# A spatial-reduction attention kernel: the query scratch in 16 rows, chunks of neighbouring tokens

## The chip, the core and the metric

The kernel runs on one core of a Trainium2 chip. The core has a matrix engine (TensorE, PE in the profile, with its weight loads as PEld), VectorE (DVE), ScalarE (ACT), GpSimd (POOL), and a queue processor (SyncE, SP) that here only issues transfers. Sixteen DMA engines move the data of the queues of SP, ACT and POOL. The metric is the time on the device in microseconds (us), of one execution. The median of three runs before is 380.58 us (380.52 to 380.81).

## What is computed

Attention of 4 x 12288 queries over 768 pooled keys per batch, followed by a mixture of eight low-rank adapters of which two are chosen for each token. The reference, cut to what matters:

```python
B, C, Hh, Ww = (4, 128, 384, 32)       # q: B x 12288 x 128, kv: B x 384 x 32 x 128
kv_pool = kv.reshape(B, H // r, r, W // r, r, C).mean(axis=(2, 4))     # r = 4
kv_flat = kv_pool.reshape(B, -1, C) @ w_sr
k = v = kv_flat                                                       # 768 keys
s = scale * (q @ k.transpose(0, 2, 1))
s = s - s.max(-1, keepdims=True)
a = np.exp(s)
a /= a.sum(-1, keepdims=True) + 1e-09
x = (a @ v)                                                           # 49152 x 128
logits = x @ w_gate                                                   # E = 8
topk = the two largest;  w = softmax over those two
out = x + sum over the two of  w * ((x @ A[e]) @ B[e])                # rank 16
```

Every token is computed by itself; the order in which tokens are taken is free, as long as each result reaches its own row of the output.

## The kernel before

**Chunks and groups.** The 49152 tokens are taken in 96 chunks `k` of T = 512 tokens, 24 per batch, and four chunks make a group `g` of GT = 2048 tokens (24 groups). A chunk has S = 4 strips of 128 tokens, the 768 keys J = 6 blocks of 128.

**Queries.** TensorE needs the queries transposed, channels on partitions: `qT[g]`, 128 x 2048 bf16. For groups 0 and 1 the queries are loaded as fp32 and turned on TensorE (`load_q`, `turn_q`). For the other 22 groups `cast_q` (L78) copies 2048 tokens from the input to a scratch tensor in DRAM, from fp32 to bf16, on POOL's queue (L80), and `load_qT` (L83) reads it back with a transposing DMA on SP's queue (L90). It sees the scratch as 128 rows `p` of 16 tokens `j` (2048 elements), so column `j*128 + p` of `qT` is token `16 p + j`. A chunk thus holds, for each of 128 partitions, four neighbouring tokens out of 16, and takes tokens from the whole group. The cast of group 4 + i is issued in the slots 8, 12, ..., 60 and in six more (`casts`, L463), the load of group g in slot 4g - 6 for g = 4 to 17, and the last six in slots 61 to 67 (`loads`, L464). A slot is one turn of the main loop, `begin(k)`; the attention of chunk k - 1 and the routing and adapters of earlier chunks are done in it. The last four groups' `qT` lie in a spare buffer (`qTs`).

**Scores.** `scores(k, r)` (L286) multiplies two blocks of keys with the chunk's 512 columns into a PSUM tile `sg` of 2 x 512, and ScalarE takes the exponential of all 1024 columns at once (L294) into `em[k]`, a tile of [128 keys, J, T] fp16. Three such units make a chunk; the main loop calls `unit()` at fixed places, somewhat more than a chunk ahead of the attention. There are two `sg` buffers.

**Attention.** `attend(k, s)` (L296) uses a strip of `em` as weights: for each of the 6 key blocks a 128 x 128 load of `em[k][:, j, s*128:(s+1)*128]` and a matmul with the extended values (136 columns) into `acc`. So the tokens of a strip come out on the partitions. `normalize` (L313), `top` and `route` choose the adapters. `attend_part` (L305) does the same in the opening, and `part` (L676) at the end.

**Adapters.** `transposes` turns x and the gated hidden values on TensorE; for the chunks in `by_dma` (68 to 89) `turn_dma` (L405) does it with transposing DMAs on SP's queue. `tanhs` runs the tanh of the routing on ScalarE (L365).

**Output.** `finish(k)` (L431) adds up and stores 256 KB on SP's queue (L434), out of one of eight `osb` buffers: 128 partitions with 2 KB each, which in the output lie 8 KB apart. At the end of the kernel, after the loop, the last chunks are stored by `add_there` (L709, two whole chunks) and `add_here` (L699, one whole chunk and four halves), the latter also on ACT's queue; both use `dest(k)` (L695).

**Order.** `keep` makes each instruction stay in program order on its engine; the queues are served in order, and waits between engines go by semaphores.

Of the kernel before, what the change touches and what calls it, by code (L numbers as in the profile page):

```python
# [11 lines left out]
BF16 = mybir.dt.bfloat16  # L12
U16 = mybir.dt.uint16
FP16 = mybir.dt.float16
AF = mybir.ActivationFunctionType
# [5 lines left out]
def kernel(  # L21
# [10 lines left out]
    nc = tc.nc  # L32
    P = 128
    B, N, C = q.tensor.shape
# [3 lines left out]
    J = NKV // P  # L38
    T = 512
    S = T // P  # L40
    GC = 4
    GT = GC * T
    VC = C + E - 1
    VE = VC + 1
    VP = 2 * C
    NB = N // T
    NCHUNK = B * NB
    scale = 1.0 / float(np.sqrt(C))
# [6 lines left out]
    ppool = ctx.enter_context(tc.tile_pool(name="ppool", bufs=8))  # L55
# [5 lines left out]
    qdram = ctx.enter_context(tc.tile_pool(name="qdram", bufs=1, space=bass.MemoryType.DRAM))  # L61
# [4 lines left out]
    keep = tc.keep_in_program_order  # L66

    def mm(*a, **k):
        return keep(nc.tensor.matmul(*a, **k))  # L69
# [5 lines left out]
    NG = N // GT  # L75
    q_bf, qT, kvr, spare = {}, {}, {}, {}

    def cast_q(g):  # L78
        t = qdram.tile([GT, C], BF16, tag=f"q{g}", name=f"qbf{g}")
        keep(nc.gpsimd.dma_start(t, q[g // NG, (g % NG) * GT:(g % NG + 1) * GT]))  # L80
        q_bf[g] = t

    def load_qT(g):  # L83
        if g < B * NG - GC:
            t = qpool.tile([P, GT], BF16, tag="qT", name="qT")
        else:
            if "q" not in spare:
                spare["q"] = kvpool.tile([P, 4, 2, 4 * C], FP32, tag="kvr", name="qTs")
            t = spare["q"][:, g % GC].rearrange("p x c -> p (x c)").bitcast(BF16)
        keep(nc.sync.dma_start(t.rearrange("c (j p) -> c j p", p=P),  # L90
                               q_bf[g].rearrange("(p j) c -> p (j c)", p=P), transpose=True))
        qT[g] = t


# [113 lines left out]
    kfT, vx = {}, {}  # L208
# [73 lines left out]
    em, acc, xn, xg, srt, gw = {}, {}, {}, {}, {}, {}  # L282
    tts, xT, hgT, hp, hg, dp = {}, {}, {}, {}, {}, {}
    R = J // 2

    def scores(k, r):  # L286
        b = k // NB
        if k not in em:
            em[k] = ppool.tile([P, J, T], FP16, tag="em", name="em")
        rhs = qT[k // GC][:, (k % GC) * T:(k % GC + 1) * T]  # L290
        ps = ps_s.tile([P, 2, T], FP32, tag="sg", name="sg")
        for i in range(2):
            mm(ps[:, i], kfT[b][:, 2 * r + i], rhs, start=True, stop=True)
        keep(nc.scalar.activation(em[k][:, 2 * r:2 * r + 2], ps, AF.Exp, bias=0.0, scale=scale))  # L294

    def attend(k, s):  # L296
        b = k // NB
        if s == 0:
            acc[k] = ps_a.tile([P, S, 256], FP32, tag="acc", name="acc")
        o = acc[k][:, s, 0:VE]  # L300
        for j in range(J):
            mm(o, em[k][:, j, s * P:(s + 1) * P], vx[b][:, j, 0:VE], start=(j == 0),
               stop=(j == J - 1))

    def attend_part(k, r):  # L305
        if r == 0:
            acc[k] = ps_a.tile([P, S, 256], FP32, tag="acc", name="acc")
        for s in range(S):
            for j in (2 * r, 2 * r + 1):
                mm(acc[k][:, s, 0:VE], em[k][:, j, s * P:(s + 1) * P], vx[k // NB][:, j, 0:VE],  # L310
                   start=(j == 0 and s % 2 == 0), stop=(j == J - 1 and s % 2 == 1))

    def normalize(k):  # L313
# [112 lines left out]
    def up(k):  # L426
        dp[k] = mtile([P, S, C], name="d_ps")
        for s in range(S):
            mm(dp[k][:, s], hgT[k][:, s], b_bf, start=(s == 0), stop=(s == S - 1))

    def finish(k):  # L431
        osb = opool.tile([P, S, C], FP32, tag="osb", name="osb")
        keep(nc.vector.tensor_tensor(osb, dp[k], xn[k][:, :, 0:C], op=ALU.add))  # L433
        keep(nc.sync.dma_start(  # L434
            out[k // GC * GT:(k // GC + 1) * GT].rearrange("(p j) c -> p j c", p=P)
            [:, k % GC * S:(k % GC + 1) * S], osb))
        for d in (em, acc, xn, xT, hgT, hp, hg, dp):
            d.pop(k, None)

# [9 lines left out]
    def cast_first():  # L449
        keep(nc.gpsimd.tensor_copy(late, q_f[1, 2][:, 0, 0:1]))  # L450
        for g in (2, 3):
            cast_q(g)
        for g in (2, 3):
            load_qT(g)
# [3 lines left out]
    def unit(k=None, r=None):  # L458
        k, r = units.pop(0 if k is None else units.index((k, r)))
        scores(k, r)  # L460
# [7 lines left out]
    def begin(k):  # L468
        nonlocal sums, rest
        b, i = divmod(k, NB)  # L470
        g = k // GC
        if k in loads:
            load_qT(loads[k])
        if k in casts:
            cast_q(4 + casts.index(k))
        if b + 1 < B:
            lo = 3 if b == 0 else 0
            if i == lo:
                sums, rest = prepare(b + 1, nc.gpsimd)
                sums = sum(sums, [])  # L480
            if lo <= i < 12 + lo:
                load_kv(b + 1, (i - lo) // 4, (i - lo) % 4, None)
        if k == 7:
            for _ in range(2):
                sums.pop(0)()
# [11 lines left out]
    enter, t, left = {}, 1, list(range(NCHUNK - 3))  # L497
# [10 lines left out]
    def step(op, *w):  # L508
        v = [int(x) if x.isdigit() else engines.get(x, pools.get(x)) for x in w]
        if op == "T":  # L510
            turn_rows(v[0], 2 * (v[2] // 2) if w[1] == "s" else v[2],
                      v[2] % 2 if w[1] == "s" else v[3])
        elif op == "turn":
            turn_q(v[0] // GC, v[0] % GC, *v[1:])
        elif op in ("keys", "keys2", "values"):
            first_rest[v[0]][("keys", "keys2", "values").index(op)]()
        elif op == "gates":
            later.pop(0)()
        else:
            {"spin": spin, "proj1": project, "proj2": project2, "sum": add_rows, "sc": unit,  # L520
             "late": cast_first, "cast": cast_weights, "slot": begin, "at": attend, "atp": attend_part,
             "norm": normalize, "top": top, "route": route, "tr": transposes, "down": down,
             "gate": gate, "up": up, "fin": finish}[op](*v)
# [23 lines left out]
    for k in range(k1, NCHUNK):  # L547
        b, i = divmod(k, NB)
# [11 lines left out]
        if kx and not kd and all(x_ in by_dma for x_ in kx):  # L560
# [16 lines left out]
            for u_ in ku:  # L577
                up(u_)
                finish(u_)
            attend(ka[0], 0)  # L580
            attend(ka[0], 1)
            unit()
            for n in kn:
# [25 lines left out]
        for u_ in ku:  # L609
            up(u_)  # L610
            finish(u_)
# [64 lines left out]
    def part(k, o, js):  # L676
        for s in range(S):
            for j in js:
                mm(o[:, s, 0:VE], em[k][:, j, s * P:(s + 1) * P], vx[k // NB][:, j, 0:VE],
                   start=(j == 0 and s % 2 == 0), stop=(j == J - 1 and s % 2 == 1))  # L680

    def wide(o):
# [9 lines left out]
        for s in range(S):  # L692
            mm(o[:, s], hgT[k][:, s], b_bf, start=(s == 0), stop=(s == S - 1))

    def dest(k):  # L695
        return out[k // GC * GT:(k // GC + 1) * GT].rearrange("(p j) c -> p j c", p=P)[
            :, k % GC * S:(k % GC + 1) * S]

    def add_here(k, lo, hi, queue):  # L699
        osb = opool.tile([P, S, C], FP32, tag="osb", name="osb")[:, 0:hi - lo]  # L700
        keep(nc.vector.tensor_tensor(osb, dp[k][:, lo:hi], xn[k][:, lo:hi, 0:C], op=ALU.add))
        keep(queue.dma_start(dest(k)[:, lo:hi], osb))

    def carry(k):
        osb = opool.tile([P, S, C], FP32, tag="osb", name="osb")
# [2 lines left out]

    def add_there(k):  # L709
        keep(nc.gpsimd.tensor_tensor(dp[k], dp[k], xn[k][:, :, 0:C], op=ALU.add))  # L710
        keep(nc.sync.dma_start(dest(k), dp[k]))

    def gate_part(k, lo, hi):
        if lo == 0:
# [8 lines left out]
    up_into(K - 4, bank(ps_m))  # L723
    o95 = bank(ps_s).rearrange("p a (b c) -> p (a b) c", c=256)
    part(K, o95, range(4))
    fetch(xT, K - 2)
    tanhs()
    down_into(K - 2, ps_m)
    carry(K - 4)
    normalize(K - 1)  # L730
    turn_x(K - 1, ps_m)
    part(K, o95, range(4, J))
    turn_h(K - 3, ps_a)
    fetch(xT, K - 1)
    top(K - 1)
    route(K - 1)
    gate_part(K - 2, 0, S)
    add_there(K - 4)

    acc[K] = o95  # L740
# [26 lines left out]
    fetch(hgT, K - 2)  # L767
    carry(K - 3)
    add_there(K - 3)
    halves = [(K, 0), (K, 2), (K - 1, 0), (K - 1, 2)]  # L770
    for k, lo in halves:
# [13 lines left out]
    for k, lo in halves:  # L785
        half(turned[k], lo, hg[k], id_bf, True)
        keep(nc.scalar.copy(hgT[k][:, lo:lo + 2], turned[k][:, lo:lo + 2]))
        if (k, lo) == (K, 2):
            half(dp[K], 0, hgT[K], b_bf, False)
            add_here(K - 2, 0, S, nc.sync)  # L790
        elif k < K:
            if lo == 0:
                half(dp[K], 2, hgT[K], b_bf, False)
                add_here(K, 0, 2, nc.sync)
                add_here(K, 2, S, nc.sync)
# [35 lines left out]
```

## Time and profile before

| | |
|---|---|
| median of the runs | 380.58 us (380.52 to 380.81, n = 3) |
| span of the profiled execution | 379.1 us |
| PE busy | 368.8 us, 97% |
| VectorE busy | 307.6 us, 81% |
| ScalarE busy | 293.3 us, 77% |
| GpSimd busy | 217.8 us, 57% |
| DMA | 82.22 MB, mean 217 GB/s |

The profile is of one execution. Its span runs from the first to the last instruction that the profiler recorded; the time of a run holds 1.5 us more. A group of instructions is shown as line, engine, operation, output<-input, number, then busy time and mean in ns, then the idle time before and what ended it. A line of the timeline has the start, the length, and what ran (neighbours of one kind are merged, xN). A line of the issues has the queue, the number, the size and the time from issue to landing.

### The profile page before, as it was taken

What the parts mean: (1) busy time and instruction counts of PE and PEld (TensorE: products, weight loads), DVE (VectorE), ACT (ScalarE), POOL (GpSimd) and SP (SyncE); (2) the same over time, 40 slices, a digit from 0 to 9 for tenths busy, and PEclk for the clock granted to TensorE, in tenths of its full rate; (3) what the DMA queues carried; (4) which work ended last, traced back from release to release, by engine and by line L of the source; (5) the groups of instructions that cost most, each with busy time, mean ns of one, the idle gap of its engine ahead of it and who ended that gap; (6) DMA issues with size and microseconds to landing.
All of it is one profiled execution on the core that took longest, in us unless ns stands there. A gap on an engine that the chain in (4) does not pass through costs nothing.

```text
span 379.1 us, 11473 instructions
## 1 busy us (share of the span) xinstructions
PE 368.8 (97%) x4448; PEld 292.5 (77%) x4448; DVE 307.6 (81%) x925; ACT 293.3 (77%) x368; POOL 217.8 (57%) x493
## 2 busy tenths in 40 slices
PE   8899999999999999999999999999999999999993
PEld 5577788788788887878788887878787777777782
DVE  1447799998989889898989888898988777777785
ACT  1448986776878788787878787777778999999873
POOL 0120468878732387777833267777675666666442
PEclk9999999999999999999999999999999999999998
DMA  7988979999999998997898998989955867777623
GB/s 247 388 291 151 279 184 266 340 224 241 152 213 228 299 278 268 255 235 165 171 201 226 288 239 245 306 233 198 217 137 140 169 163 153 150 205 168 141 86 140
DMA packets 93863, 82.22 MB, mean 217 GB/s; under 512 B 73104, under 2 KB 73872, under 8 KB 93456
## 3 DMA queue, kind: packets, MB, share of 16 engines
q1 hardware_dynamic: 92672, 69.75, 69.8%
q0 software_dynamic: 704, 11.54, 17.0%
q8 instruction: 35, 0.57, 0.6%
q10 hardware_dynamic: 432, 0.20, 0.2%
q14 instruction: 20, 0.16, 0.2%
HBM read 50.53 MB, written 36.70 MB: 230 GB/s over the span
## 4 chain that ended last, share of the span: by engine, by line
PE 91%; DMA 4%; DVE 2%; issue 1%; ACT 1%; SPq 0%; POOL 0%; ACTq 0%; DVEq 0%; POOLq 0%
PE acc L69 35%; PE sg L69 32%; PE tt_ps L69 8%; PE d_ps L69 5%; PE h_ps L69 5%; DMA kvr<-in_kv_dram 4%; PE kpT_ps L69 2%; PE v_ps L69 1%; DVE kvr L135 1%; DVE xn L320 1%; PE kfT_ps L69 1%; DMA out_dram<-osb 1%; PE qT_ps L69 0%; SPq L102 0%; PE tail_ps L69 0%
## 5 line engine op out<-in xcount | busy, mean ns | idle before, releaser
L294 ACT ACTIVATE em<-sg 128x1024 f16<-128x1024 f32 x288 | 282.4, 1022 | 66.8 <-PE sg L69 64.1
L69 PE MATMUL acc<-vx,em 128*128 128x136 f16 x2280 | 166.5, 223 | 0.0
L69 PEld LDWEIGHTS <-em 128*128 128x128 f16 x2304 | 145.2, 98 | 7.7 <-DVE xn L320 0.4
L69 PE MATMUL sg<-qT,kfT 128*128 128x512 bf16 x480 | 142.1, 379 | 0.8 <-ACT em L294 0.7
L320 DVE TENSOR_TENSOR xn<-acc,rinv 128x540 f32<-128x540 f32 x95 | 68.4, 720 | 3.3
L69 PEld LDWEIGHTS <-tts 128*128 128x128 bf16 x564 | 43.0, 98 | 31.6 <-issue 0.4
L223 POOL TENSOR_TENSOR kvr<-kvr 128x512 f32<-128x512 f32 x54 | 67.3, 1270 | 0.1
L352 POOL TENSOR_TENSOR over<-xn,srt 128x64 f32<-128x64 f32 (+1 forms) x120 | 30.9, 278 | 55.4 <-DVE srt L340 55.3
L433 DVE TENSOR_TENSOR osb<-d_ps,xn 128x512 f32<-128x512 f32 x91 | 62.5, 688 | 0.0
L420 DVE TENSOR_TENSOR hg<-h_ps,gw 128x512 bf16<-128x512 f32 x71 | 49.0, 691 | 6.3 <-POOL gw L368 1.2
L389 DVE COPY tts<-tt_ps 128x1024 bf16<-128x1024 bf16 (+1 forms) x73 | 49.0, 672 | 0.0
L69 PEld LDWEIGHTS <-kfT 128*128 128x128 bf16 x576 | 45.3, 98 | 2.7 <-issue 1.0
L315 DVE RECIPROCAL rinv<-acc 128x4 f32<-128x4 f32 x95 | 17.3, 182 | 36.9 <-PE acc L69 35.9
L367 POOL TENSOR_TENSOR gw<-th,over 128x64 f32<-128x64 f32 (+1 forms) x60 | 17.3, 288 | 49.6 <-ACT th L365 47.4
L69 PEld LDWEIGHTS <-xn 128*128 128x128 bf16 x296 | 22.5, 98 | 16.7 <-DVE xn L320 0.4
L340 DVE MAX8 srt<-xn 128x8 f32<-128x8 f32 x380 | 34.4, 152 | 0.1
L69 PE MATMUL sg<-qTs,kfT 128*128 128x512 bf16 x96 | 28.6, 379 | 0.0
L69 PE MATMUL tt_ps<-id_bf,xn 128*128 128x128 bf16 x284 | 27.4, 219 | 0.0
L69 PE MATMUL h_ps<-a_bf,tts 128*128 128x128 bf16 x284 | 27.4, 219 | 0.0
L69 PE MATMUL tt_ps<-id_bf,hg 128*128 128x128 bf16 x280 | 27.1, 219 | 0.0
L69 PE MATMUL d_ps<-b_bf,tts 128*128 128x128 bf16 x276 | 26.7, 219 | 0.1
L358 POOL TENSOR_SCALAR over<-over 128x64 f32<-128x64 f32 (+1 forms) x60 | 19.8, 330 | 5.4
(93 smaller groups left out, 280.7 us busy)
## 6 DMA issues: line engine op xcount, KB each, us to landing
out_dram<-osb SPq DMA_DIRECT2D x94, 256.0 KB, 4.3
kvr<-in_kv_dram SPq DMA_DIRECT2D x45, 512.0 KB, 7.8
qbf<-in_q_dram POOLq DMA_DIRECT2D x22, 512.0 KB, 7.7
qf<-in_q_dram SPq DMA_DIRECT2D x8, 256.0 KB, 7.4
kvr<-in_kv_dram SPq DMA_DIRECT2D x6, 256.0 KB, 7.8
out_dram<-osb SPq DMA_DIRECT2D x3, 128.0 KB, 2.3
turn<-turn SPq DMA_TRANSPOSE x23, 3.1
qT<-qbf SPq DMA_TRANSPOSE x18, 7.4
```

Of the source, the lines that this page charges most:

```text
L69: return keep(nc.tensor.matmul(*a, **k))
L223: keep(adder.tensor_tensor(u[:, lo:hi], u[:, lo:hi], v[:, lo:hi], op=ALU.add))
L294: keep(nc.scalar.activation(em[k][:, 2 * r:2 * r + 2], ps, AF.Exp, bias=0.0, scale=scale))
L315: keep(nc.vector.reciprocal(ri, acc[k][:, :, VC]))
L320: keep(nc.vector.tensor_tensor(x[:, :, 0:VC], acc[k][:, :, 0:VC], ri.unsqueeze(2).broadcast_to([P, S, VC]), op=ALU.mult))
L340: keep(nc.vector.max(srt[k0][:, m, s], xn[k][:, s, C:C + E]))
L352: keep(eng.tensor_tensor(d, lg, so[:, :, i].unsqueeze(2).broadcast_to([P, n, 8]), op=ALU.subtract))
L358: keep(eng.tensor_scalar(mask, mask, 0.0, None, op0=ALU.is_ge))
L367: keep(eng.tensor_tensor(w[:, 0:n], th, mask, op=ALU.mult))
L389: keep(nc.vector.tensor_copy(sb[:, lo:hi], ps[:, lo:hi]))
L420: keep(nc.vector.tensor_tensor(hg[k].rearrange("p s (e r) -> p (s e) r", e=E), hp[k].rearrange("p s (e r) -> p (s e) r", e=E), gw[k0][:, m ...
L433: keep(nc.vector.tensor_tensor(osb, dp[k], xn[k][:, :, 0:C], op=ALU.add))
```

## The change

Three things go together, for groups 2 to 23 (chunks 8 to 95).

The scratch tensor of a group has 16 rows `r`. Row r holds, for each of the four chunks m of the group, 32 neighbouring tokens (8 KB in bf16): token `512 m + 32 r + x` of the group. The transposing DMA reads the 16 rows as they are, so column `512 m + 16 x + r` of `qT` is that token, and a chunk is 512 neighbouring tokens.

`em[k]` is laid out as [keys, strip, key block, 128]. The exponential reads the scores in another order: with `x = 4 u + s`, strip s takes the columns `64 u + 16 s + r`, in runs of 16. A strip's partition `16 u + r` is then token `32 r + 4 u + s` of the chunk, so a partition has four neighbouring tokens in its four strips. In groups 0 and 1 the strips are read as before, in runs of 128.

The store (a new function `store`, used for all outputs) writes 128 runs of 2 KB into the chunk's own 256 KB of the output, in the order u, r; groups 0 and 1 are stored as before.

```diff
     def cast_q(g):
-        t = qdram.tile([GT, C], BF16, tag=f"q{g}", name=f"qbf{g}")
-        keep(nc.gpsimd.dma_start(t, q[g // NG, (g % NG) * GT:(g % NG + 1) * GT]))
+        t = qdram.tile([16, GT // 16 * C], BF16, tag=f"q{g}", name=f"qbf{g}")
+        src = q[g // NG, (g % NG) * GT:(g % NG + 1) * GT]
+        keep(nc.gpsimd.dma_start(t.rearrange("r (m x) -> r m x", m=GC),
+                                 src.rearrange("(m r x) c -> r m (x c)", r=16, m=GC)))
         q_bf[g] = t
...
-        keep(nc.sync.dma_start(t.rearrange("c (j p) -> c j p", p=P),
-                               q_bf[g].rearrange("(p j) c -> p (j c)", p=P), transpose=True))
+        keep(nc.sync.dma_start(t.rearrange("c (i r) -> c i r", r=16), q_bf[g], transpose=True))
...
     def scores(k, r):
         b = k // NB
         if k not in em:
-            em[k] = ppool.tile([P, J, T], FP16, tag="em", name="em")
+            em[k] = ppool.tile([P, S, J, P], FP16, tag="em", name="em")
...
-        keep(nc.scalar.activation(em[k][:, 2 * r:2 * r + 2], ps, AF.Exp, bias=0.0, scale=scale))
+        o = em[k][:, :, 2 * r:2 * r + 2]
+        if k // GC > 1:
+            o = o.rearrange("p s i (u r) -> p s (i u) r", r=16)
+            i_ = ps.rearrange("p i (u s r) -> p s (i u) r", s=S, r=16)
+        else:
+            i_ = ps.rearrange("p i (s t) -> p s i t", s=S)
+        keep(nc.scalar.activation(o, i_, AF.Exp, bias=0.0, scale=scale))
...
-            mm(o, em[k][:, j, s * P:(s + 1) * P], vx[b][:, j, 0:VE], start=(j == 0),
+            mm(o, em[k][:, s, j], vx[b][:, j, 0:VE], start=(j == 0),
                stop=(j == J - 1))
...
+    def store(queue, k, osb, lo=0, hi=S):
+        if k // GC < 2:
+            to = out[k // GC * GT:(k // GC + 1) * GT].rearrange("(p j) c -> p j c", p=P)
+            keep(queue.dma_start(to[:, k % GC * S + lo:k % GC * S + hi], osb))
+            return
+        to = out[k * T:(k + 1) * T].rearrange("(r u s) c -> u r s c", r=16, s=S)[:, :, lo:hi]
+        keep(queue.dma_start(to, osb))
+
     def finish(k):
         osb = opool.tile([P, S, C], FP32, tag="osb", name="osb")
         keep(nc.vector.tensor_tensor(osb, dp[k], xn[k][:, :, 0:C], op=ALU.add))
-        keep(nc.sync.dma_start(
-            out[k // GC * GT:(k // GC + 1) * GT].rearrange("(p j) c -> p j c", p=P)
-            [:, k % GC * S:(k % GC + 1) * S], osb))
+        store(nc.sync, k, osb)
```

The other reads of `em` (`attend_part`, `part`) and the other stores (`add_here`, `add_there`) change in the same way.

More of the change, by code (lines that the diff above doesn't have):

```diff
@@ L309, in attend_part @@
             for j in (2 * r, 2 * r + 1):
-                mm(acc[k][:, s, 0:VE], em[k][:, j, s * P:(s + 1) * P], vx[k // NB][:, j, 0:VE],
+                mm(acc[k][:, s, 0:VE], em[k][:, s, j], vx[k // NB][:, j, 0:VE],
                    start=(j == 0 and s % 2 == 0), stop=(j == J - 1 and s % 2 == 1))
@@ L678, in part @@
             for j in js:
-                mm(o[:, s, 0:VE], em[k][:, j, s * P:(s + 1) * P], vx[k // NB][:, j, 0:VE],
+                mm(o[:, s, 0:VE], em[k][:, s, j], vx[k // NB][:, j, 0:VE],
                    start=(j == 0 and s % 2 == 0), stop=(j == J - 1 and s % 2 == 1))
@@ L693, in up_into @@
             mm(o[:, s], hgT[k][:, s], b_bf, start=(s == 0), stop=(s == S - 1))
-    def dest(k):
-        return out[k // GC * GT:(k // GC + 1) * GT].rearrange("(p j) c -> p j c", p=P)[
-            :, k % GC * S:(k % GC + 1) * S]
     def add_here(k, lo, hi, queue):
@@ L701, in add_here @@
         keep(nc.vector.tensor_tensor(osb, dp[k][:, lo:hi], xn[k][:, lo:hi, 0:C], op=ALU.add))
-        keep(queue.dma_start(dest(k)[:, lo:hi], osb))
+        store(queue, k, osb, lo, hi)
     def carry(k):
@@ L710, in add_there @@
         keep(nc.gpsimd.tensor_tensor(dp[k], dp[k], xn[k][:, :, 0:C], op=ALU.add))
-        keep(nc.sync.dma_start(dest(k), dp[k]))
+        store(nc.sync, k, dp[k])
     def gate_part(k, lo, hi):
```

## The prediction

> **What bounds the kernel now.** The page first: busy times, chain, queues.
>
> ```profile
> PE 368.8 (97%) x4448; PEld 292.5 (77%) x4448; DVE 307.6 (81%) x925; ACT 293.3 (77%) x368; POOL 217.8 (57%) x493
> ...
> q1 hardware_dynamic: 92672, 69.75, 69.8%
> q0 software_dynamic: 704, 11.54, 17.0%
> ...
> q10 hardware_dynamic: 432, 0.20, 0.2%
> ...
> PE 91%; DMA 4%; DVE 2%; issue 1%; ACT 1%; SPq 0%; POOL 0%; ACTq 0%; DVEq 0%; POOLq 0%
> ...
> L294 ACT ACTIVATE em<-sg 128x1024 f16<-128x1024 f32 x288 | 282.4, 1022 | 66.8 <-PE sg L69 64.1
> ...
> out_dram<-osb SPq DMA_DIRECT2D x94, 256.0 KB, 4.3
> kvr<-in_kv_dram SPq DMA_DIRECT2D x45, 512.0 KB, 7.8
> qbf<-in_q_dram POOLq DMA_DIRECT2D x22, 512.0 KB, 7.7
> ...
> out_dram<-osb SPq DMA_DIRECT2D x3, 128.0 KB, 2.3
> turn<-turn SPq DMA_TRANSPOSE x23, 3.1
> qT<-qbf SPq DMA_TRANSPOSE x18, 7.4
> ```
>
> TensorE is busy 97% of the span and carries 91% of the chain. But the average hides the stages, so next the windows. The columns are the window, its length, then PE, PEld, DVE, ACT and POOL busy, the granted clock, the DMA share and GB/s.
>
> ```profile
> 60.00:140.00 80.00, 80.00 (x1020) 64.94 (x1018) 72.03 (x209) 60.94 (x75) 50.46 (x96) 1.00 1.01 238
> 140.00:250.00 110.00, 110.00 (x1395) 89.09 (x1393) 98.08 (x285) 86.62 (x104) 71.63 (x132) 1.00 0.98 239
> 250.00:280.00 30.00, 30.00 (x381) 24.28 (x379) 26.82 (x77) 23.40 (x28) 21.42 (x37) 1.00 1.08 223
> 285.00:350.00 65.00, 64.92 (x785) 50.36 (x783) 49.63 (x165) 61.63 (x81) 42.29 (x141) 1.00 0.73 165
> ```
>
> From 60 to 350 us PE has next to no idle time (0.08 us), at full clock: nothing that only shortens another engine's work can gain there. Two other columns are nearly full. [...] ACT is at 95% in the last stage, where transposes have moved from PE to DMA. Whether ACT sets that stage is read from its timeline, in both stages.
>
> ```profile
> 149.70 2.86 ACT L294 ACTIVATE em<-sg 128x1024 f16<-128x1024 f32 x3 [0.61 <-PE sg L69]
> ...
> 305.75 0.22 ACT L365 ACTIVATE th<-over 128x32 f32<-128x32 f32 x1
> 305.87 3.15 ACT L294 ACTIVATE em<-sg 128x1024 f16<-128x1024 f32 x3
> 308.91 0.22 ACT L365 ACTIVATE th<-over 128x32 f32<-128x32 f32 x1
> ```
>
> Three exps run back to back in 2.86 us, but are spread over 3.15 in the last stage; its period, tanh to tanh, is 308.91 - 305.75 = 3.16. Back to back an exp follows the one before after (2.86 - 1.02) / 2 = 0.92 us, and the tanh delays one by 0.12 (305.75 to 305.87). So ACT needs 3 x 0.92 + 0.12 = 2.9 of 3.16 us: PE paces this stage too, and an exp may grow by some 0.08 us before ACT takes over.
>
> The chain gives the period (a slot) of the earlier stages, from one chunk's last matmuls to the next's: 3.61 us.
>
> ```profile
> 81.29 1.07 PE acc L69 x18
> 84.90 1.07 PE acc L69 x18
> ```
>
> **The change part by part.**
>
> *Exp in permuted order* (264 of 288 exps read runs of 16 scores; the first 24 read runs of 128). The element count stays 1024, so the base price is the same 1022 ns. ACT has no row with short runs. The nearest are DVE's:
>
> ```profile
> L433 DVE TENSOR_TENSOR osb<-d_ps,xn 128x512 f32<-128x512 f32 x91 | 62.5, 688 | 0.0
> L420 DVE TENSOR_TENSOR hg<-h_ps,gw 128x512 bf16<-128x512 f32 x71 | 49.0, 691 | 6.3 <-POOL gw L368 1.2
> ```
>
> L420 reads an operand that steps every 16 elements and costs 3 ns more than L433, which has runs of 128. The lower bound is 0 (no element is dropped, so a gain is excluded). For the upper bound let each of the 64 breaks between runs cost as much as three elements: 64 x 3 x 1022/1024 = 0.19 us. I take 0, as L420 shows. It costs nothing up to the 0.08 us above.
>
> *The em layout* keeps the same 128 contiguous fp16 columns per weight load and the same matmuls: 0.
>
> *Cast and transpose of the queries.* The cast stays 512 KB, in runs of 8 KB. Before, 704 packets over 22 casts are 32 each, which is 16 of 32 KB and 16 that close the transfer; now 64 and 16. POOL's issue takes:
>
> ```profile
> L80 POOL DMA_DIRECT2D qbf<-in_q_dram x22: 504/577/755, 27.0 to 242.4; - x22
> ```
>
> Between 0 and twice 577 ns for four times the pieces; I take 0.1 us. POOL idles 28 of the 80 us in the first window, so a cast in every fourth slot of 3.6 us hides; without that cover the gates of one chunk would come 0.6 us later. The transpose moves the same blocks of 16 x 128, now from one 16-row stripe with each row contiguous. Its landing may halve (3.7 us) or double (15 us); I take 7.4. A group is loaded at slot 4g - 6 and its chunk 4g is scored near slot 4g - 1, so five slots, 18 us, cover it; only past 18 us would PE wait. SP issues one transpose for one: no queue order changes.
>
> *The stores.* This is where I see a price. The SBUF side keeps 128 partitions of 2 KB. The DRAM side was 128 rows; it becomes u r (s c): 8 by 16 runs of 2 KB, outermost count 8. What do the transfers before tell? ACT's queue has three transfers of 128 rows each (w_sr, w_gate, half of an output chunk) and 432 packets = 3 x (128 + 16): 16 closing packets each, one for each DMA engine. With the casts above, every transfer that I can count uses 16 engines, and the outermost counts in the code are 16, 32 or 128. None has 8. If transfers are dealt out by the outermost dimension, a new store uses 8 engines, each with 16 packets in place of 8.
>
> The Trainium skill, "DMA: Bandwidth & Descriptors", section "Why a DMA increments its semaphore by 16 and not by 1", states such a rule: the number of engines is the largest up to 16 that divides the slowest dimension of both sides. By that rule it is 8 here; no run so far shows it.
>
> What it costs depends on who waits. In the body nobody does: eight osb buffers at 3.6 us are 28 us against 4.3. The end of the kernel does wait:
>
> ```profile
> 371.00:373.00 2.00, 1.27 (x15) 0.93 (x16) 1.75 (x6) 1.42 (x4) 0.94 (x2) 1.00 0.36 139
> 374.20:377.40 3.20, 0.27 (x2) 0.19 (x2) 1.10 (x4) 0.22 (x1) 0.00 (x0) 0.70 0.91 328
> ...
> 370.55 3.20 SPq L711 DMA_DIRECT2D out_dram<-osb  x2
> 373.84 2.18 SPq L702 DMA_DIRECT2D out_dram<-osb  x4
> 374.90 0.38 ACTq L702 DMA_DIRECT2D out_dram<-osb  x1
> ```
>
> The first window holds one 256 KB store: 0.36 x 2.0 = 0.72 us of all engines, 1.44 of eight. The second holds the last six: 328 GB/s x 3.2 us is 1.05 MB, two of 256 KB and four of 128 KB. They keep the engines busy 0.91 x 3.2 = 2.9 us, back to back behind the issues. On eight engines that is 5.8 us. Less about 0.1 us of the gaps that they now fill, the end moves by **+2.8 us**.
>
> *SP's issues.* A store with three dimensions may take the longer form of the kvr load:
>
> ```profile
> L434 SPq DMA_DIRECT2D out_dram<-osb x91: 332/529/3993, 48.5 to 365.2; - x91
> ...
> L102 SPq DMA_DIRECT2D kvr<-in_kv_dram x45: 534/589/3370, 0.7 to 243.2; - x45
> ```
>
> 534 - 332 = 0.2 us more at the least. SP waits for osb most of the time, and in the tail the engines' backlog hides it; alone it would add 0.2 us once. Bounds 0 and 0.2; I take 0.
>
> **Sum.** The profiled execution has a span of 379.1; the runs have a median of 380.58, so 1.5 lies outside the span and stays. 379.1 + 2.8 = 381.9, and 380.58 + 2.8 = **383.4 us**, with a range of its own of 382.4 to 384.6 (eight engines, dispatch of the last six a little looser or tighter).
>
> **The rivals.**
>
> *A: the backlog reaches PE at the entry to the last stage.* With half the engines each store adds 0.72 us to engines that already carry a share of 1.0. SP's timeline there:
>
> ```profile
> 268.15 4.11 SPq L90 DMA_TRANSPOSE qT<-qbf  x1
> 272.36 0.53 SPq L434 DMA_DIRECT2D out_dram<-osb  x1
> 272.98 3.17 SPq L90 DMA_TRANSPOSE qTs<-qbf  x1
> 276.24 2.57 SPq L434 DMA_DIRECT2D out_dram<-osb  x3
> 283.51 1.20 SPq L407 DMA_TRANSPOSE turn<-turn  x1
> ...
> L69 PEld LDWEIGHTS <-turn x176: 95/98/98, 288.1 to 360.5; 128*128 128x128 bf16 x176
> ```
>
> From 250 to 280 the share is 1.08, query transposes and nine stores with no pause. Nine times 0.72 is 6.5 us more work: the last transpose would be done near 284 in place of 278, and the first turned chunk, issued at 283.5 and landing 3.1 later at 286.6, would come near 291. PE reads it at 288.1, 1.5 after it lands, so it would wait about 3 to 5 us. Time: 383.4 + 4.5 = 387.9. For it: the full share. Against it: shares over 1 show that the engines are not at their limit, and the transposes run in slots of 3.6 us that leave room.
>
> *B: sixteen engines, exp as before: no change.* Then every edit is hidden and only SP's 0.2 us stays: 380.58 + 0 to 0.2, that is 380.6 to 380.8. This is also the case in which the change of layout doesn't do anything that the clock sees. For it: PE's full windows, and that 16 runs per u could be dealt out too. Against it: the counts above, where the outermost dimension always explains 16.
>
> *C: exp grows past its cushion.* At the upper bound of 0.19 us an exp exceeds 0.08 by 0.11; three per period and 20 periods in the last stage (65 / 3.16) give 6.6 us, so 387.2 with 16 engines. It decides from 0.08 us on; below that it is nothing. In the earlier stages (3.61 - 2.9) / 3 = 0.24 us per exp stay free, so C stays in the last one. For it: 64 breaks per read and a change of bank eight times as often. Against it: DVE's 3 ns.
>
> *D: faster.* The last stores now fill one stretch of DRAM each. If that cut their landing of 2.3 us by half, with 16 engines, the end would come 1.1 us earlier: 379.5. Nothing else can gain, PE having no idle time from 60 to 350. Against it: the store's time is packets of 2 KB, and these stay.
>
> **How the numbers follow.** The counts of packets speak for dealing by the outermost dimension, but nothing in the trace has an outermost 8, so I give eight engines 0.66: the forecast 0.50 and A 0.16. B 0.18, C 0.10, D 0.06. The forecast is the likeliest, 383.4. The range goes down to B (380.4, the lower runs before being at 380.5) and up past A to 388.6; it leaves out D and the far ends of A and C, some 0.15. A measurement of this kernel can tell about 0.2% (0.76 us) from no change. Faster by more than that: D, 0.06. Within it: B, 0.18. Slower: forecast, A and C, 0.76.
>
> **What would show it.** Eight engines: the packets of q1 fall by 8 closing ones for each of the 89 changed stores of SP's 97 (the first eight chunks keep their form), from 92672 to 91960, and q10 from 432 to 424; with sixteen both stay. The last window of the stores, 3.2 us at a share of 0.91, becomes nearly twice as long at half the share. Exp's mean stays at 1022 ns, or C begins; above 1100 it decides. q0 goes to 22 x 80 = 1760 packets. The period of the last stage stays 3.16. In A, PE would show a gap behind a DMA between 283 and 295, and the DMA share near 284 would no longer fall. The prediction is wrong if q1 keeps its packets, or if PE waits anywhere between 60 and 280, or if the final stores' backlog is not what ends the kernel.

## The result, and the profile after

| | before | after |
|---|---|---|
| median of the runs beside each other | 380.65 us (380.52 to 380.81, n = 4) | 398.86 us (398.63 to 400.09, n = 4) |
| ratio | | 1.0486, interval 1.0471 to 1.0501 |
| span of the profiled execution | 379.1 us | 398.3 us |
| forecast | | 383.4 us, range 380.4 to 388.6 |

The change costs 18.2 us. The direction was forecast; the size lies far outside the range. First the page of the changed kernel: busy times, queues, chain, and the costliest group.

```profile
span 398.3 us, 11473 instructions
...
PE 371.3 (93%) x4448; PEld 292.8 (74%) x4448; DVE 308.3 (77%) x925; ACT 294.0 (74%) x368; POOL 217.6 (55%) x493
...
q1 hardware_dynamic: 47256, 69.74, 69.9%
q0 software_dynamic: 1760, 11.54, 16.3%
...
q10 hardware_dynamic: 424, 0.20, 0.2%
...
PE 84%; DMA 8%; DVE 3%; ACT 1%; issue 1%; SPq 0%; POOL 0%; ACTq 0%; DVEq 0%; POOLq 0%
...
L301 ACT ACTIVATE em<-sg 128x1024 f16<-128x1024 f32 x288 | 282.7, 1022 | 81.0 <-PE sg L69 78.4
```

The work on the engines is nearly what it was (PE 371.3 us against 368.8, exp still 1022 ns). The span grew by waiting: the DMA's share of the chain rose from 4% to 8%. Before, no wait of PE for a turned chunk was on record; now the table of waits (what waited, for what; total, times, longest) has two kinds.

```profile
PEld L69 <- DMA turn<-turn: 14.5, 8, 7.9
...
PE h_ps L69 <- DMA turn<-turn: 10.6, 3, 7.4
```

The windows say where. First the kernel before at the entry to the last stage, then the changed one:

```profile
280.00:290.00 10.00, 9.92 (x122) 7.73 (x120) 9.04 (x26) 7.35 (x11) 5.11 (x17) 1.00 0.24 58
290.00:300.00 10.00, 10.00 (x125) 7.87 (x123) 7.54 (x26) 9.27 (x13) 6.42 (x22) 1.00 0.78 156
```

```profile
140.00:250.00 110.00, 110.00 (x1396) 89.07 (x1395) 98.27 (x286) 86.87 (x105) 71.22 (x131) 1.00 0.97 239
250.00:280.00 30.00, 30.00 (x382) 24.28 (x380) 26.86 (x79) 23.56 (x29) 21.41 (x37) 1.00 0.92 166
280.00:290.00 10.00, 8.93 (x109) 6.89 (x106) 8.33 (x24) 6.94 (x11) 5.20 (x17) 1.00 0.72 138
290.00:300.00 10.00, 3.67 (x27) 3.08 (x28) 1.99 (x7) 1.19 (x3) 0.92 (x5) 0.71 0.75 158
```

Until 280 us PE is as full as before; nothing is lost there. But the DMA rate from 250 to 280 has fallen from 223 to 166 GB/s, at a share of 0.92 against 1.08: less is moved, and yet the share, read as load, would say that the engines have more room. The bill comes at 288 us, when PE needs the first turned chunk. The columns of PE's timeline are start, length, instructions, and the idle time before with its releaser:

```profile
288.34 0.59 PE L69 MATMUL sg<-qT,kfT 128*128 128x512 bf16 x2
296.33 0.61 PE L69 MATMUL h_ps<-a_bf,turn 128*128 128x128 bf16 x4 [7.40 <-DMA turn<-turn]
```

One row of the tile of the turned chunks measures the delay in any kernel: when PE first and last uses such a chunk. Before and after:

```profile
L69 PE MATMUL h_ps<-a_bf,turn x88: 219/219/219, 288.4 to 354.6; 128*128 128x128 bf16 x88
```

```profile
L69 PE MATMUL h_ps<-a_bf,turn x88: 219/219/314, 296.3 to 369.3; 128*128 128x128 bf16 x88
```

So the 19.2 us of the span split into 7.9 by the first use (296.3 - 288.4), 6.8 more by the last (14.7 - 7.9) and 4.5 after it.

Why the first chunk is late is read from SP's queue, from the six last query transposes on:

```profile
256.93 4.54 SPq L92 DMA_TRANSPOSE qT<-qbf  x1
...
277.83 4.71 SPq L92 DMA_TRANSPOSE qT<-qbf  x1
282.64 0.60 SPq L444 DMA_DIRECT2D out_dram<-osb  x1
283.34 4.52 SPq L92 DMA_TRANSPOSE qTs<-qbf  x1
287.95 2.21 SPq L444 DMA_DIRECT2D out_dram<-osb  x3
290.26 3.13 SPq L414 DMA_TRANSPOSE turn<-turn  x1
```

Between the first and the sixth of these transposes one transpose with one store takes (283.34 - 256.93) / 5 = 5.28 us. Before, the sixth was issued at 272.98, and the first at:

```profile
253.53 2.88 SPq L90 DMA_TRANSPOSE qT<-qbf  x1
```

That is 3.89 us each. The last of the six is issued 10.4 us later than before (283.34 against 272.98): 3.4 us of it stood already at the first of the six (256.93 against 253.53), and 7.0 grew over these five pairs. The single packets of the DMA engines show what happens in that time (start and end in us, bytes, number, median ns of one). The changed kernel first, one store and one transpose in steady state and then the entry to the last stage; below it the kernel before:

```
after   268.01-271.66   2048 n=128 med 84      store
        268.80-272.98  32768 n=6   med 4105    transpose
        269.52-272.98  32768 n=2   med 3452
        270.75-273.09  32768 n=8   med 1671
        287.54-289.06  32768 n=3   med 1420    the last query transpose's last packets
        289.19-300.10   2048 n=640 med 84      five stores
        292.87-297.94    256 n=1024 med 18     two turned chunks between them
before  271.25-271.96   2048 n=128 med 84      store
        271.90-273.77    256 n=2048 med 18     transpose
        274.40-277.75    256 n=2048 med 18     the last query transpose
        284.69-285.46    256 n=512 med 18      the first turned chunk
```

A query transpose is now sixteen packets of 32 KB, one for each engine. Eight of them start while the store is still on the other eight engines, and yet all sixteen end together, from 272.94 to 273.09; the last one to start, at 271.67, is done in 1.42 us, the first ones take 4.1. The other five of these six transposes show the same: each ends 1.42 us after its last packet has started, and that packet starts when the store's last one ends. So the engines that a store has left free spend the time inside a transpose packet that does not end before the rest. Store and transpose thus stand one behind the other, and the last query transpose ends at 289.06 instead of 277.75, 11.3 us later. Five stores have queued up behind it, and the first turned chunk passes among those. A store here takes 3.65 us (268.01 to 271.66) while transpose packets run beside it; a lone one takes less, as the table of outermost counts below shows, and why it takes longer here stays open.

### The profile page after: what moved, and what is told of

It is laid out like the page before. It is cut to its first block, busy times and chain, and to the rows that moved or that the text cites. A ratio compares the mean times of both kernels' runs of the same rounds, so it can differ in the third digit from the quotient of the medians.

```text
span 398.3 us, 11473 instructions
## 1 busy us (share of the span) xinstructions
PE 371.3 (93%) x4448; PEld 292.8 (74%) x4448; DVE 308.3 (77%) x925; ACT 294.0 (74%) x368; POOL 217.6 (55%) x493
## 3 DMA queue, kind: packets, MB, share of 16 engines
q1 hardware_dynamic: 47256, 69.74, 69.9%
q0 software_dynamic: 1760, 11.54, 16.3%
## 4 chain that ended last, share of the span: by engine, by line
PE 84%; DMA 8%; DVE 3%; ACT 1%; issue 1%; SPq 0%; POOL 0%; ACTq 0%; DVEq 0%; POOLq 0%
PE acc L69 33%; PE sg L69 29%; PE tt_ps L69 8%; PE h_ps L69 5%; PE d_ps L69 5%; DMA turn<-turn 5%; DMA kvr<-in_kv_dram 3%; PE kpT_ps L69 2%; PE v_ps L69 1%; DVE xn L327 1%; DVE kvr L136 1%; PE kfT_ps L69 1%; ACT em L301 0%; PE tail_ps L69 0%; DVE turn L427 0%
## 5 line engine op out<-in xcount | busy, mean ns | idle before, releaser
L301 ACT ACTIVATE em<-sg 128x1024 f16<-128x1024 f32 x288 | 282.7, 1022 | 81.0 <-PE sg L69 78.4
L69 PEld LDWEIGHTS <-turn 128*128 128x128 bf16 x176 | 12.9, 98 | 23.1 <-DMA turn<-turn 14.5
```

The lines of the kernel that those rows point to most:

```text
L301: keep(nc.scalar.activation(o, i_, AF.Exp, bias=0.0, scale=scale))
```

## The experiments

The question was which of three things costs the time: the stores on eight engines, the place in DRAM that they write, or the scratch. The expectations stand as written before each run. In the kernels that change the store without the scratch, or the other way round, rows reach other places within their chunk's or group's part of the output; the bytes and instructions are those of the whole work. The median of before beside the runs was 380.62 to 380.78. The labels e1 to e9 are those by which the expectations refer to each other.

**e1: the new stores alone, in the kernel before.**

```diff
+    def store(queue, k, osb, lo=0, hi=S):
...
+        to = out[k * T:(k + 1) * T].rearrange("(r u s) c -> u r s c", r=16, s=S)[:, :, lo:hi]
+        keep(queue.dma_start(to, osb))
...
```

> The kernel before with the changed stores alone; each chunk's rows land in another order within its own 256 KB of the output. Theory 1 (stores on 8 engines are the whole cost, through the queue of the engines that they fill): 394 to 400 us, about the changed kernel's 398.9, with PE waiting on a turn DMA at the entry of the last stage, and q1 712 packets short. Theory 2 (the query transposes, now one 32 KB packet on each engine that all end together, are the cost; the stores only cost the tail): 383 to 384 us, no PE wait before the tail.

Measured: 406.3, 425.72, 432.19 and 437.58 us, more than the whole change. Even the shortest of the four, which is the one profiled, lies above all of the changed kernel's. All four lie above the 394 to 400 us that were expected. The queue, then the waits, of the profiled execution:

```profile
q1 hardware_dynamic: 91960, 69.74, 76.7%
```

```profile
PEld L69 <- DMA turn<-turn: 20.3, 6, 13.3
...
PE h_ps L69 <- DMA turn<-turn: 17.8, 4, 12.8
```

712 packets fewer than before, as for eight engines. The wait is of the same kind as in the changed kernel, and longer. So the stores are enough to cause it, and none of the four runs shows the rest of the change making it worse. Why the four runs spread over 31 us stays open.

**e2: the change with its stores flat over 128 partitions.**

```diff
-        to = out[k * T:(k + 1) * T].rearrange("(r u s) c -> u r s c", r=16, s=S)[:, :, lo:hi]
+        to = out[k * T:(k + 1) * T].rearrange("(p s) c -> p s c", s=S)[:, lo:hi]
```

> The changed kernel, but each chunk stored as 128 partitions in order (outermost count 128), so that its rows land in another order within its own 256 KB. Theory 1: 380 to 381 us, q10 back at 432 packets, no PE wait at the entry. Theory 2: 394 us or more, PE still waits there.

Measured: 381.06 us (380.43 to 381.53, n = 10), ratio 1.0003 (0.9982 to 1.0025). Queues and windows:

```profile
q1 hardware_dynamic: 47968, 69.75, 63.4%
...
q10 hardware_dynamic: 432, 0.20, 0.2%
```

```profile
140.00:250.00 110.00, 110.00 (x1397) 89.10 (x1394) 98.28 (x286) 86.92 (x105) 71.38 (x132) 1.00 0.91 231
250.00:280.00 30.00, 30.00 (x382) 24.26 (x380) 26.85 (x78) 23.50 (x29) 21.51 (x37) 1.00 0.86 229
...
366.00:367.50 1.50, 1.50 (x30) 1.50 (x28) 1.19 (x3) 1.07 (x2) 0.84 (x4) 1.00 0.45 175
```

One line takes all of the 18 us away. The 712 closing packets are back, and no wait of PE for a turned chunk is left. Exp order, em layout, cast and transpose cost nothing that can be measured. They do shorten the pair of a transpose and a store: from the first to the sixth of the last transposes (issued at 254.60 and 271.88) it takes 3.46 us here and 3.89 before. But PE has no idle time for that to fill. The last window holds one store by itself: its packets run from 366.36 to 367.18, 0.82 us.

**e3: the scratch in runs of 1 KB, with that flat store.** Each token now goes to the partition that the flat store expects.

```diff
-        keep(nc.gpsimd.dma_start(t.rearrange("r (m x) -> r m x", m=GC),
-                                 src.rearrange("(m r x) c -> r m (x c)", r=16, m=GC)))
+        keep(nc.gpsimd.dma_start(t.rearrange("r (m u x) -> r m u x", m=GC, u=8),
+                                 src.rearrange("(m u r s) c -> r m u (s c)", m=GC, u=8, r=16)))
```

> The changed kernel with the scratch rows filled in runs of 1 KB (four neighbouring tokens in every 64), so that partition p of a chunk holds tokens 4p to 4p+3 and the store is one flat block with outermost count 128. The cast has 512 pieces in place of 64. Theory 1: 380 to 381.5 us, the casts landing later than 8 us but hidden; POOL's issue longer than 0.58 us. Theory 2: as e2, 394 us or more.

Measured: 381.12 us (380.69 to 381.75, n = 10), ratio 1.0005 (0.9986 to 1.0024). The cast's issues on POOL, after the change and here:

```profile
L81 POOL DMA_DIRECT2D qbf<-in_q_dram x22: 527/559/729, 27.3 to 242.8; - x22
```

```profile
L81 POOL DMA_DIRECT2D qbf<-in_q_dram x22: 644/696/866, 26.3 to 242.5; - x22
```

Each cast now has 512 data packets and 16 closing ones in place of 64 and 16 (q0 counts 11616 = 22 x 528). At the median POOL pays 0.14 us more for an issue, and nothing of it is seen in the time.

**e4 to e6: the new stores in one stage at a time**, flat elsewhere: only the last five chunks (e4, k > 90), only the body (e5, k < 68), only the last stage (e6, 68 to 90). The edit of e4 is shown; the other two differ in the condition alone.

```diff
-        to = out[k * T:(k + 1) * T].rearrange("(r u s) c -> u r s c", r=16, s=S)[:, :, lo:hi]
+        if k > 90:
+            to = out[k * T:(k + 1) * T].rearrange("(r u s) c -> u r s c", r=16, s=S)[:, :, lo:hi]
+        else:
+            to = out[k * T:(k + 1) * T].rearrange("(p s) c -> p s c", s=S)[:, lo:hi]
```

> The changed kernel with the new stores only for the last five chunks (91 to 95), flat ones for the others (their rows in another order). The term of the forecast: 380.6 + 2.8 = 383.4. From the changed kernel's tail, where a store of 256 KB takes 2.1 to 2.5 us on the engines and not 1.4, theory 1 gives 380.6 + 4 to 5 = 385 us. Theory 2: 395 us or more.

> The changed kernel with the new stores only for chunks 8 to 67, flat ones after (rows in another order). If the backlog of the query transposes at 250 to 290 us is what stalls PE at the entry of the last stage, this run has the stall of the changed kernel there (its first scores of chunk 76 came 10.0 us later than before): 389 to 391 us. If the stall needs the new stores in the last stage too (rival): under 384 us.

> The changed kernel with the new stores only for chunks 68 to 90 (rows of the others in another order). Of the changed kernel's loss 4.6 us came between chunk 76 and chunk 92. If these stalls belong to the last stage by itself: 383.5 to 386 us. If they are only the echo of the late entry (rival): 380.5 to 381.5 us.

| new stores in | median | against before | ratio |
|---|---|---|---|
| the tail | 385.38 us (n = 4) | +4.8 | 1.0109 (1.0063 to 1.0154) |
| the body | 391.45 us (n = 4) | +10.7 | 1.0277 (1.0234 to 1.0321) |
| the last stage | 383.23 us (381.41 to 386.34, n = 10) | +2.5 | 1.0068 (1.0037 to 1.0099) |

The sum is 18.0 us, and the change costs 18.2. The three parts add up to all of it, within intervals of 1.2 to 1.7 us on each. Against what was expected e5 lies 0.5 us high and e6 0.3 us low, both clear of their rivals. The row of the first and last use, in the same order:

```profile
L69 PE MATMUL h_ps<-a_bf,turn x88: 219/219/219, 288.8 to 355.1; 128*128 128x128 bf16 x88
```

```profile
L69 PE MATMUL h_ps<-a_bf,turn x88: 219/219/314, 296.2 to 364.5; 128*128 128x128 bf16 x88
```

```profile
L69 PE MATMUL h_ps<-a_bf,turn x88: 219/219/230, 288.4 to 357.2; 128*128 128x128 bf16 x88
```

With new stores in the body alone, PE's first use is already 7.8 us late though the last stage's own stores are flat; by the last use it is 9.9. The waits of that kernel are one event (PE and its weight load at the same moment); those with the new stores in the last stage are many small ones:

```profile
PEld L69 <- DMA turn<-turn: 7.9, 1, 7.9
...
PE h_ps L69 <- DMA turn<-turn: 7.4, 1, 7.4
```

```profile
PEld L69 <- DMA turn<-turn: 5.7, 10, 1.4
```

In the tail PE waits for nothing new; the transfers end later. The last stores' packets with flat stores (e2), and with new ones in the tail (e4):

```
flat    371.75-372.57  2048 n=128   374.61-376.17  2048 n=256   376.00-377.69  1024 n=512
tail    372.42-379.33  2048 n=384                               378.68-382.34  1024 n=512
```

Three stores of 256 KB take 6.9 us on end, 2.3 each, and the end comes 4.65 us later.

**e7: eight engines, 32 KB in a row for each.** This keeps the outermost 8 and takes the scatter in DRAM away.

```diff
-        to = out[k * T:(k + 1) * T].rearrange("(r u s) c -> u r s c", r=16, s=S)[:, :, lo:hi]
+        to = out[k // GC * GT:(k // GC + 1) * GT].rearrange(
+            "(u m r s) c -> m u r s c", u=8, m=GC, r=16)[k % GC][:, :, lo:hi]
```

> The changed kernel with stores of the same outermost count 8, but each of the 8 writes 32 KB in one piece, 128 KB from the next (rows in another order). If the number of engines is the cause: 394 to 402 us, q1 again 712 packets short. If the scatter in DRAM (steps of 16 KB on one engine, neighbours 2 KB apart) makes a store take 2.1 to 2.5 us in place of 1.4 (rival): 385 to 391 us, and a lone store near 1.4 us.

**e8: sixteen engines, scattered.** The outermost count is 16, and an engine's runs of 2 KB lie 32 KB apart.

```diff
+        to = out[k * T:(k + 1) * T].rearrange("(b a s) c -> a b s c", a=16, s=S)[:, :, lo:hi]
```

> The changed kernel with stores of outermost count 16, scattered in DRAM as before it: neighbours 2 KB apart, an engine's own runs 32 KB apart (rows in another order). If the number of engines is the cause: 380.5 to 381.5 us, q10 432. If the scatter is (rival): over 385 us.

**e9: sixteen engines, 16 KB in a row for each.** The same instruction form as the last one, without its scatter.

```diff
+        to = out[k // GC * GT:(k // GC + 1) * GT].rearrange(
+            "(a m b s) c -> m a b s c", a=16, m=GC, b=8)[k % GC][:, :, lo:hi]
```

> The changed kernel with stores of outermost count 16 in the three-dimension form, each engine writing 16 KB in one piece (rows in another order). e8 cost 1.4 us more than the flat store, and its lone store took 1.28 us where the flat one took 0.82. If that is the scatter in DRAM: 380.6 to 381.2 us and a lone store near 0.82 us. If it is the form of the store, or which partitions an engine gets (rival): 381.8 to 382.5 us and 1.28 us again; then a store on 8 engines at 2.5 us is twice this 1.28 and not twice 0.72.

| outermost, bytes in a row | median | ratio | one store by itself |
|---|---|---|---|
| 8, 2 KB (the change) | 398.86 us | 1.0486 (1.0471 to 1.0501) | 2.5 us |
| 8, 32 KB | 398.23 us | 1.045 (1.041 to 1.049) | 2.5 and 2.7 us |
| 16, 2 KB | 382.11 us | 1.0028 (1.0013 to 1.0043) | 1.28 us |
| 16, 16 KB | 382.08 us | 1.0037 (1.0022 to 1.0051) | 1.3 us |
| 128, 2 KB (flat) | 381.06 us | 1.0003 (0.9982 to 1.0025) | 0.82 us |

The packets of e7 and then of e8 by the queues' rows, with the wait for turned chunks of e7 (in e8 it is 0.2 us in all):

```profile
q1 hardware_dynamic: 47256, 69.74, 70.4%
...
q10 hardware_dynamic: 424, 0.20, 0.2%
...
PEld L69 <- DMA turn<-turn: 14.2, 11, 7.5
```

```profile
q1 hardware_dynamic: 47968, 69.75, 66.8%
...
q10 hardware_dynamic: 432, 0.20, 0.2%
```

The number of engines decides, and the place in DRAM does not: long rows leave the cost with eight engines and change nothing with sixteen. A second, small price shows beside it, and puts e8 0.6 us above the 380.5 to 381.5 expected of it. A store with a three-dimensional DRAM side takes 1.3 us on sixteen engines where the flat one takes 0.82, and the kernels with it take about 1 us longer than the flat one. What in it takes the time (which partitions an engine is given, or the making of its descriptors) was not tried and stays open.

None of these kernels is faster than the kernel before.

## Why the prediction was wrong

**What held.** PE bounds the kernel and is full from 60 to 280 us. Exp in permuted order costs 0 (1022 ns), and rival C falls with it. em's layout, the cast and the transpose are hidden: the flat store shows all of them together at a ratio of 1.0003. q10 fell to 424 and q0 rose to 1760 as forecast, and the eight engines are there: 712 fewer closing packets, as the flat store brings them back. The Trainium skill, "DMA: Bandwidth & Descriptors", section "Why a DMA increments its semaphore by 16 and not by 1", lets the slowest dimension of both sides choose the number of engines; the traces now agree for the DRAM side, with 424 and 432 packets on q10 for an outermost 8 and 16.

**The first step that failed: "In the body nobody does [wait]".** That compared a store's landing with the eight osb buffers, which is right as far as it goes, but osb is not the only thing behind a store on SP's queue. The query transposes are behind it too, and the turned chunks behind those. The mechanism was then named, as rival A, and set aside at 0.16; the sign written down for A, a gap of PE behind a DMA between 283 and 295, is the one that came. The reason against it was that "shares over 1 show that the engines are not at their limit"; the share cannot show that, as an engine inside a waiting transpose packet counts as busy: in the changed kernel the share fell to 0.92 while the backlog grew. Nor was a share over 1 a sign of room in the kernel before. From 250 to 280 SP's queue alone made up the 1.08 there, so packets of this one queue overlapped in time, and the sum of their times does not tell how full the engines were. The other reason, that transposes in slots of 3.6 us leave room, fell too: with its store a transpose took 3.89 us on average even before, and 5.28 after.

**A's price was mis-sized as well.** It took nine stores times 0.72 = 6.5 us of more work, and a wait of 3 to 5 us. Measured: the last query transpose 11.3 us later, PE's first use 7.9 us later, and the body alone +10.7. The working spread a store's extra time evenly over engines that could go on meanwhile; in the records the transpose cannot end until its last engine is free. And it gave a stall no price beyond its own length. These two windows of the changed kernel are from behind the stall:

```profile
299.00:300.00 1.00, 1.00 (x10) 0.96 (x9) 0.66 (x5) 0.28 (x1) 0.26 (x2) 0.50 0.52 157
301.00:301.50 0.50, 0.50 (x11) 0.50 (x10) 0.00 (x0) 0.50 (x1) 0.00 (x0) 0.99 0.99 179
```

PE ran at half clock from its restart at 296.33 until about 301: 4.7 us at half, some 2 us more. That is the step from 7.8 to 9.9 in the kernel with new stores in the body alone (e5). There PE restarts at 296.18, and its second use of a turned chunk comes at 301.89 against 291.98 before: 9.9 us late already, and no later at the last use. The Trainium skill, "TensorE: Matmul & The Clock Gate", section "Part 1: The HAM clock gate", has such a half clock after at least one idle window, and at least one busy window of about 3.4 us before it is left. The trace agrees on the half, and its 4.7 us are more than one such window.

**The tail's term, 2.8 us, was mis-sized:** measured +4.8. The mechanism was right: the same bytes on half the engines take longer, and the last stores end the kernel. But it doubled 0.72 us to 1.44, and a lone store on eight engines takes 2.5 to 2.7 us: twice the 1.28 of the three-dimensional form, not twice the flat one's 0.82. So the packets of the last six stores run for 7.3 us (389.40 to 396.70) where they ran for 3.0 before (374.25 to 377.29), and the working had 5.8 for 2.9. That the form has a price of its own was not in the working; only its issue was (0.2 us more, forecast 534 ns, measured 603 at the least):

```profile
L444 SPq DMA_DIRECT2D out_dram<-osb x89: 603/607/1589, 79.2 to 391.7; - x89
```

**The last stage was not in the sum at all.** Each turned chunk follows a store on the queue there as well; ten waits of up to 1.4 us give +2.5.

**"The transpose moves the same blocks of 16 x 128" was wrong in form.** Its packets went from 256 bytes to 32 KB: q1 fell not to 91960 but to 47256, which is 91960 - 22 x 2048 + 22 x 16. It took nothing from the time, since with flat stores nobody was waiting for it, and it shows how a count can be right in one part (the 712) and miss another that is over sixty times larger.

**The chances.** Eight engines had 0.66, and within it the case that decided had 0.16 against 0.50. By the terms now measured, the forecast's own case would have come to 380.6 + 4.8 = 385.4, with A's 10.7 to 396.1, with the last stage to 398.6. In the forecast the direction rested on the tail's term alone, and that is 4.8 of the 18.2 us.

## What to carry to other kernels

Keep the outermost dimension of a store's DRAM side a multiple of 16 (here 16 and 128 used all sixteen engines, and 8 did not), and check it by the closing packets in the queue's count: one line of a store's access pattern was worth 4.9% here. Price a transfer that loads the engines unevenly where its queue is fullest and not only where it ends the kernel; on a queue that also carries DMA transposes, count it as serial with them. And when TensorE has no slack and is to wait for several us (7.4 here), add the half clock after the wait to the wait itself.

## What the runs showed of the hardware

A DMA transpose from a scratch of 16 rows moves as sixteen packets of 32 KB, from 128 rows as 2048 packets of 256 bytes. A packet of 32 KB that started last took 1.42 us; in the kernel before, one transpose's 2048 packets ran from 271.90 to 273.77, 1.87 us. In the changed kernel all sixteen end within 0.15 us of each other, though their starts lie 2.9 us apart.

With the old transposes the stores on eight engines did more harm than with the new ones: 406.3 us in the shortest of four runs against 400.1 in the longest of four. What in the old transposes does it was not tried.
